# GpSimd instead of SP waits for the two result stores at the end of a decode kernel

## The chip, the core and the metric

The kernel runs on one core of one Trainium2 chip. A core has five engines with an instruction stream each: TensorE (PE; its weight loads are listed apart as PEld), VectorE (DVE), ScalarE (ACT), GpSimd (POOL) and SyncE (SP). They meet only at semaphores. Transfers are run by 16 DMA engines, and are issued here by SP and by ACT.

The metric is the device time of one execution, in microseconds (us). It covers a little more than the span of the profile, which goes from the first to the last instruction of the program: what the runtime does on every engine ahead of the program and behind it lies outside of the span.

## What is computed

One token goes through an attention block with a sliding window and, beside it, through a two-layer perceptron; both results and the input are added.

```python
xn = layernorm(x)                                   # x: 1 x 1024
q  = (xn @ wq) -> 32 heads x 128                    # wq: 1024 x 4096
k, v = last 4096 rows of the caches                 # 4 KV heads x 128, each shared by 8 heads
p  = softmax(q k^T / sqrt(128));  o = p v           # 32 heads
A  = o @ wo                                         # wo: 4096 x 1024
B  = gelu(layernorm(xn) @ w1 + b1) @ w2 + b2        # w1: 1024 x 3584, w2: 3584 x 1024
out = x + A + B                                     # 1 x 1024, bf16
```

## The kernel before

All weights and the part of the caches that is needed, 39.86 MB, are read once. SP issues these large loads; ACT issues the three small ones (b1, x and b2) at the start. Each load has a semaphore of its own, and each engine counts its results in a semaphore (the `Track` objects `PE`, `DVE`, `ACT`, `POOL`); a consumer waits for a count. There is no scheduler: the order of the work is the order in which the function writes it down, engine by engine.

In order of time: the small loads and the layer norms; the first perceptron layer as w1 lands; the gelu; the transposition of K on DVE; the queries as wq lands; scores, softmax and the second perceptron layer; the product with V; last, the output projection as wo lands. wo comes in four pieces of 20, 8, 3 and 1 of 32 columns of chunks (`WO_CHUNKS`), so that little is left to compute when the last piece has landed. All contributions to the result (x, b2, the perceptron, the attention) add up in one bank of PSUM as four quarter rows of 256.

GpSimd works at the start: constants, masks, a few products for the layer norms. Its last instruction (line 561) multiplies the sums of the softmax. From there to the end of the program its stream is empty.

The end (lines 621 to 631) works like this. The last matmul counts up the semaphore of PE (`C["fin"]`). PE ends with a branch at line 623 that is never taken. ACT waits for that count and copies the result out of PSUM to `ORow` as bf16 (line 627). Then ACT and SP each wait for ACT's count and each issue one store of 1 KB, half of the result; both stores add 16 to the semaphore `s_out` when they have landed (lines 628 to 630). SP then waits until `s_out` is 32 (line 631). This is the last instruction of the program on any engine.

Of the kernel before, what the change touches and what calls it, by code (L numbers as in the profile page):

```python
# [52 lines left out]
def bass_parallel_sum__sliding_block_cached__mixer_channel_mlp__decode_kernel(  # L53
# [18 lines left out]
    pe, dve, act, pool, sp = nc.tensor, nc.vector, nc.scalar, nc.gpsimd, nc.sync  # L72

    def sems(name, n):
        return [nc.alloc_semaphore(f"{name}{i}") for i in range(n)]

    s_xrow, s_b1, s_b2, s_w1, s_w2, s_out, s_go, s_row = (
        nc.alloc_semaphore(n) for n in ("s_xrow", "s_b1", "s_b2", "s_w1", "s_w2", "s_out", "s_go", "s_row"))
# [549 lines left out]
    for g, eng in enumerate((act, sp)):  # L628
        eng.wait_ge(ACT.sem, C["a_out"])
        eng.dma_start(out_rows[2 * g:2 * g + 2, :], ORow[31 + 64 * g:33 + 64 * g, :]).then_inc(s_out, 16)  # L630
    sp.wait_ge(s_out, 32)

    return nc

# [27 lines left out]
```

## Time and profile before

Three runs gave 99.16, 98.95 and 99.00 us, the median is 99.0 us. The profiled execution took 99.08 us.

| what | value |
|---|---|
| profiled execution, its own time | 99.08 us |
| its span, first to last instruction | 97.6 us (97.559) |
| outside of the span | 1.52 us |
| bytes read | 39.86 MB, 409 GB/s over the span |
| DMA's share of the chain that ended last | 88% |
| last matmuls on PE, start | 95.49 us |
| copy of the result on ACT, start and length | 95.81 us, 0.38 us |
| issue of the two stores, start and length | 96.22 us, 0.33 us on SP and 0.27 us on ACT |
| SP's wait for the stores | 1.0 us |
| last instruction on GpSimd, start and length | 72.24 us, 0.66 us |

The span ends with SP's wait. Semaphore instructions are not counted as busy, so the last microsecond looks empty in the table of busy time: only the list of SP's own waits shows it.

### The profile page before, as it was taken

The page shows a single profiled execution, that of the slowest core. Times are in us where ns is not written, and L with a number is a line of the kernel's source. Part 1 is how long each engine was busy: PE and PEld are TensorE (multiplying, and loading weights), DVE is VectorE, ACT ScalarE, POOL GpSimd, SP SyncE. Part 2 cuts the span into 40 slices and gives each one's busy share as a digit, 9 for nine tenths or more (in the row PEclk, how much of TensorE's full clock was granted, in tenths as well). Part 3 has the DMA queues.
Part 4 walks back from the last instruction along what each step waited for, and adds up shares of the span by engine and source line. Part 5 has one row for each costly group of instructions (what it writes and reads, how often), then busy time and mean ns, then how long its engine had stood idle before and what let it go on. Part 6 is the DMA issues. An engine that isn't in the chain of part 4 may idle for free.

```text
span 97.6 us, 1308 instructions
## 1 busy us (share of the span) xinstructions
PE 45.9 (47%) x527; PEld 19.8 (20%) x445; DVE 32.3 (33%) x43; ACT 12.3 (13%) x27; POOL 11.0 (11%) x31
## 2 busy tenths in 40 slices
PE   0000022649660000000069839993896499926962
PEld 0000022213120000000012122212544257603530
DVE  0000003270049999999900140416490000200000
ACT  0500000240320000000000130017680000100001
POOL 2000001499950000000000000000020000000000
PEclk9999999999998555555555799999579966997599
DMA  9798888999999999999898888999999699699980
GB/s 376 329 426 376 377 376 377 470 430 443 430 537 457 430 457 511 430 457 457 380 400 376 376 376 376 541 427 430 430 430 484 285 521 521 285 396 437 394 332 1
DMA packets 1340, 39.86 MB, mean 409 GB/s; under 512 B 182, under 2 KB 186, under 8 KB 444
## 3 DMA queue, kind: packets, MB, share of 16 engines
q1 hardware_dynamic: 1300, 39.85, 95.4%
q10 hardware_dynamic: 40, 0.01, 0.1%
HBM read 39.86 MB, written 0.00 MB: 409 GB/s over the span
## 4 chain that ended last, share of the span: by engine, by line
DMA 88%; PE 7%; SPq 2%; issue 1%; ACT 0%
DMA WW<-in_A_wq_dram 48%; DMA WW<-in_A_wo_dram 39%; PE PS L336 7%; SPq L199 1%; SPq L206 1%; SPq L214 0%; ACT ORow L627 0%; SPq L372 0%
## 5 line engine op out<-in xcount | busy, mean ns | idle before, releaser
L328 DVE STREAM_TRANSPOSE KV<-KV 128x2048 bf16<-128x2048 bf16 x8 | 18.5, 2312 | 0.3
L336 PE MATMUL PS<-WW,XNTb 128*32 x64 | 6.2, 574 | 20.3 <-SPq L372 20.3
L336 PE MATMUL PS<-WW,VEC 128*32 (+1 forms) x240 | 11.3, 337 | 4.6 <-SPq L610 3.1
L336 PEld LDWEIGHTS PS<-WW,VEC 128*32 (+1 forms) x236 | 6.0, 112 | 9.8 <-issue 8.8
L336 PE MATMUL PS<-KV,LB 128*128 128x512 bf16 x32 | 7.5, 386 | 0.7 <-DVE LB L452 0.7
L291 PE MATMUL PS<-oneb,XBR 1*128 1x1 bf16 x8 | 0.6, 194 | 13.8 <-DMA XBR<-in_A_x_dram 13.8
L336 PE MATMUL PS<-KV 128*64 x64 | 5.9, 345 | 2.1 <-DMA KV<-in_A_v_cache_dram 1.7
L336 PEld LDWEIGHTS PS<-WW,XNTb 128*32 x32 | 1.3, 126 | 25.5 <-issue 25.5
L336 PE MATMUL PS<-WW,YTb 128*32 x56 | 5.3, 507 | 1.6 <-DMA WW<-in_B_w_dram 1.6
L561 POOL TENSOR_TENSOR SUMX<-SAME,SUMP 128x128 f32<-128x128 f32 x1 | 0.7, 660 | 43.9 <-DVE SUMP L548 43.9
L294 DVE COPY XT<-PS 128x8 f32<-128x8 f32 x1 | 0.2, 168 | 14.4 <-PE PS L291 14.4
L336 PEld LDWEIGHTS PS<-KV 128*64 x64 | 3.9, 134 | 3.9 <-issue 3.3
L427 ACT ACTIVATE Hs<-PS 128x512 bf16<-128x512 f32 x1 | 0.6, 597 | 26.9 <-PE PS L336 26.9
L496 DVE TENSOR_REDUCE MXP<-PS 128x1 f32<-128x1024 f32 x2 | 2.4, 1224 | 4.5 <-PE PS L336 4.5
L592 DVE SCALAR_TENSOR_TENSOR OD<-PS,BLK,OD 128x128 f32<-128x128 f32 x1 | 0.3, 350 | 10.4 <-ACT OD L589 10.4
L291 PEld LDWEIGHTS PS<-oneb,XBR 1*128 1x128 bf16 x8 | 0.6, 160 | 13.8 <-issue 13.8
L429 DVE CAST Hs<-PS 128x512 bf16<-128x512 f32 x1 | 0.7, 691 | 7.2 <-PE PS L336 7.2
L545 DVE STREAM_TRANSPOSE KV<-KV 128x1024 bf16<-128x1024 bf16 x2 | 2.4, 1224 | 1.9 <-ACT KV L516 1.9
L516 ACT ACTIVATE KV<-PS,BIAS 128x512 bf16<-128x512 f32 x4 | 2.7, 682 | 0.1
L336 PEld LDWEIGHTS PS<-WW,YTb 128*32 x32 | 1.6, 111 | 5.6 <-issue 5.0
L336 PEld LDWEIGHTS PS<-KV,LB 128*128 128x128 bf16 x16 | 1.5, 96 | 5.6 <-issue 4.7
L221 POOL TENSOR_SCALAR_AFFINE_SELECT OUTM<-OUTM 2x512 bf16<-2x512 bf16 x1 | 2.3, 2303 | 0.1
(95 smaller groups left out, 42.3 us busy)
## 6 DMA issues: line engine op xcount, KB each, us to landing
WW<-in_B_w_dram SPq DMA_DIRECT2D x2, 7168.0 KB, 29.7
WW<-in_A_wo_dram SPq DMA_DIRECT2D x1, 5120.0 KB, 32.2
KV<-in_A_k_cache_dram SPq DMA_DIRECT2D x1, 4096.0 KB, 28.6
KV<-in_A_v_cache_dram SPq DMA_DIRECT2D x1, 4096.0 KB, 49.4
WW<-in_A_wo_dram SPq DMA_DIRECT2D x1, 2048.0 KB, 36.8
WW<-in_A_wo_dram SPq DMA_DIRECT2D x1, 768.0 KB, 38.2
WW<-in_A_wo_dram SPq DMA_DIRECT2D x1, 256.0 KB, 38.3
KV<-in_B_b_dram ACTq DMA_DIRECT2D x1, 7.0 KB, 8.8
```

The source lines that it names most:

```text
L199: sp.dma_start(dst[:, c0 * width:(c0 + n) * width].rearrange("p (c n) -> p c n", c=n), src[:, c0:c0 + n, :],).then_inc(semaphores[j], 16)
L206: sp.dma_start(dst[:, :], cache[0, :, SK - W:SK, :].rearrange("g (m b) d -> m g (b d)", m=MB),).then_inc(semaphore, 16)
L221: return POOL.mark(pool.affine_select(out=out, in_=out, pattern=pattern, compare_op=op, fill=value, base=base, channel_multiplier=step))
L291: last = pe.matmul(xt[:, r:r + 1], lhsT=XBR[0:1, r:D:KC], rhs=oneb[0:1, 0:1])
L328: C["kd"] = DVE.mark(dve.transpose(out=KD4[:, n], in_=KR[:, n * 2048:(n + 1) * 2048].rearrange("p (b e s) -> p b e s", b=16, e=4)))
L336: return pe.add_instruction(mybir.InstMatmult(name=nc.get_next_instruction_name(), engine=pe.engine, ins=[lowered(rhs, False), lowered(lhs ...
L427: C["a_qs"] = ACT.mark(act.activation(out=Qs[:, 0:512], in_=PS[:, 6 * 512:7 * 512], func=ACTF.Copy))
L429: C["d_qs"] = DVE.mark(dve.tensor_copy(Qs[:, 512:1024], PS[:, 7 * 512:8 * 512]))
L496: C["mx", i] = DVE.mark(dve.tensor_reduce(out=MXP[:, i:i + 1], in_=PS[:, i * 1024:(i + 1) * 1024], axis=AX.X, op=ALU.max))
L516: C["exp", n] = ACT.mark(act.activation(out=Pb[:, n * 512:(n + 1) * 512], in_=PS[:, n * 512:(n + 1) * 512], func=ACTF.Exp, bias=BIAS[:, i: ...
L545: C["tr", half] = DVE.mark(dve.transpose(out=PT[:, half * 1024:(half + 1) * 1024].rearrange("p (b m i g) -> p b m i g", b=HB, i=2, g=2), i ...
L561: C["sumx"] = POOL.mark(pool.tensor_tensor(out=SUMX[:, :].rearrange("p (g r) -> p g r", g=2), in0=SAME[:, :].unsqueeze(1).to_broadcast([12 ...
```

## The change

The instruction that waits until both stores have landed moves from SP's stream to GpSimd's. SP and ACT issue their stores as before. SP's stream now ends with the issue of its store (line 630), and GpSimd's, which ended with line 561, ends with the wait.

```diff
     for g, eng in enumerate((act, sp)):
         eng.wait_ge(ACT.sem, C["a_out"])
         eng.dma_start(out_rows[2 * g:2 * g + 2, :], ORow[31 + 64 * g:33 + 64 * g, :]).then_inc(s_out, 16)
-    sp.wait_ge(s_out, 32)
+    pool.wait_ge(s_out, 32)
 
     return nc
```

## The prediction

> **What bounds the kernel now.** I read the chain that ended last first. It says what the kernel is made of: 88% of it is the transfers of wq and wo, and at its end stand the last four matmuls and ACT's copy of the result.
>
> ```profile
> 57.13 38.31 DMA WW<-in_A_wo_dram
> 95.44 0.04 issue
> 95.49 0.30 PE PS L336 x4
> 95.78 0.02 issue
> 95.81 0.38 ACT ORow L627
> ```
>
> Nothing of this is touched. All that the change touches lies behind 96.2 us, so I read the order of events from 95 us on.
>
> ```profile
> 95.49 0.27 PE L336 MATMUL PS<-WW,VEC 128*32 128x256 bf16 x4
> 95.81 0.38 ACT L627 ACTIVATE ORow<-PS 128x256 bf16<-128x256 f32 x1 [12.35 <-PE PS L336]
> 96.22 0.33 SPq L630 DMA_DIRECT2D out_dram<-ORow  x1
> 96.22 0.27 ACTq L630 DMA_DIRECT2D out_dram<-ORow  x1
> ```
>
> The last row there starts at 96.22, the span ends at 97.56: the rest is a wait, which only SP's own list of waits shows, with its instruction under line 631.
>
> ```profile
> SPq L631 <- DMA out_dram<-ORow: 1.0, 1, 1.0
> ```
>
> ```profile
> L631 SPq EVENT_SEMAPHORE  x1: 17/17/17, 97.5 to 97.5; - x1
> ```
>
> So the span ends 17 ns after SP noticed that the stores had landed. GpSimd's list of waits shows it idle long before (its last instruction starts at 72.24 us):
>
> ```profile
> POOL SUMX L561 <- DVE SUMP L548: 43.9, 1, 43.9
> ```
>
> What follows the wait is outside of the span, but inside of the time: 99.08 - 97.56 = 1.52 us. No view prints it. The trace does keep the time of every write to a semaphore, and one semaphore that the program doesn't use (number 2) is counted up nine times in three rounds: just ahead of the first instruction, behind the last, and once more. These are rounds in which the engines meet. In us from the span's start:
>
> | step | ahead of the program | behind it | last round |
> |---|---|---|---|
> | 1 | -0.370 | 95.941 | 98.635 |
> | 2 | -0.336 | 96.849 | 98.669 |
> | 3 | -0.298 | 96.887 | 98.708 |
> | 4 | -0.254 | 96.931 | 98.752 |
> | 5 | -0.230 | 97.684 | 98.775 |
> | 6 | -0.119 | 97.727 | 98.873 |
> | 7 | -0.080 | 97.765 | 98.911 |
> | 8 | -0.046 | 97.799 | 98.945 |
> | 9 | 0.000 | 97.847 | 98.992 |
>
> The middle column tells who is who. Step 1 comes right after PE's last matmul has counted (95.78), step 2 after ACT's issue, steps 3 and 4 at once after it, by engines that had nothing left to do (POOL and DVE); then all stop until step 5, 0.125 us after SP's wait ended. Nine steps by five engines are a way up and a way down: PE, ACT, POOL, DVE, SP, DVE, POOL, ACT, PE. That POOL is third and DVE fourth I infer: semaphores are reset behind this round in five blocks, one per engine, and the blocks that start first after steps 6 and 7 are 156 to 206 and 105 to 155, ordered like the steps. From step 9 to the end of the last round is 1.145 us of resets and a second meeting. The last step, 98.99, lies 0.09 us short of the 99.08 us of this execution, so the time ends with this round, and whatever delays step 9 of the middle round delays the time.
>
> **The change part by part.**
>
> *Removed from SP.* SP's stream ends with the issue of its store (96.22 + 0.33 = 96.55). ACT, whose issue ends at 96.48, reaches its step at 96.85, 0.37 us later; SP likewise would be ready at about 96.92, 0.6 us ahead of the landing. SP comes off the path. Nothing is queued behind the wait on SP, and no DMA moves: both stores are issued as before, on the same two queues. Taken alone, this removes the SP tail: the wait's start is 17 ns after the last landing (97.525 to 97.542), step 5 comes 142 ns after that.
>
> *Added to POOL.* One semaphore instruction. Nothing of the program is queued behind it, and its place in the stream, behind line 561, is reached at 72.9 us: no engine waits for anything of POOL's after that. But its step 3 of the meeting is now late, and with it all behind it.
>
> *What is late next: the way through the meeting.* Before, the landing releases SP at the turning point; from step 5 to step 9 it takes 97.847 - 97.684 = 0.163 us. After, it releases POOL at step 3, and the count must go up to SP and down again. A round in which all are ready shows steps 3 to 9: 0.298 us ahead of the program (-0.298 to 0), 0.284 us in the last round (98.708 to 98.992). The difference is 0.121 to 0.135; I take the middle, 0.128 us. Most of it is the turn: step 5 to 6 takes 0.043 where DVE has been waiting (middle column), but 0.098 to 0.111 where the count comes straight up.
>
> The Trainium skill, page "Runtime: NRT & Kernel Launch", section "The launch sequence", gives this meeting as a serpentine over five engines with about 44 ns a hop. Released at step 3 in place of step 5, the count has two more hops to go: by that page an estimate of 0.088 us, and a sum smaller by 0.04 us. The trace's whole rounds of eight hops (0.370 and 0.357 us) agree with the page; its middle round, where a waiting DVE answers in 0.043 us, doesn't have the dear turn, and so I go by the trace.
>
> *What POOL itself needs.* Its tail, from the landing to its step, is not in this trace. Three parts by the nearest rows, in each case POOL against SP:
> - noticing: a POOL semaphore instruction in line 230 starts 32 ns after the DVE write it waits for (17.025 against 16.993), SP's 17 ns after the landing: +0.015.
> - going on to the next instruction: two such instructions of POOL in the preparation of the program follow each other by 79 ns; SP goes from its one there to its first DMA in 83 ns. No difference, or up to +0.03 if two instructions follow and SP's 142 ns hold two of 58: I take +0.015.
> - a drain, if each engine drains before it meets the others. SP's in the preparation takes 7 ns. POOL's takes 187 ns:
>
> ```profile
> L647 SPq DRAIN  x1: 7/7/7, 0.0 to 0.0; - x1
> L647 POOLq DRAIN  x1: 187/187/187, 0.4 to 0.4; - x1
> L647 POOL MEMSET const-uint8-127<- x1: 120/120/120, 0.4 to 0.4; 128x1 uint8 x1
> ```
>
> That drain waits for the memset, which starts at 0.39 and ends at 0.51; the drain ends at 0.56, some 0.05 behind it. With POOL long idle, the cost lies between SP's 0.007 and the whole 0.187; I take the 0.05 that it needs beyond the work it waits for, so +0.043 over SP.
>
> Could POOL be quicker than SP? Ahead of the program POOL starts its first instruction 0.215 us after its step 7, SP 0.230 after its step 5: -0.015 is the low end for the tail. The high end is 0.015 + 0.03 + 0.18 = +0.225.
>
> *Sum.* 0.128 (way) + 0.015 + 0.015 + 0.043 (tail) = +0.20 us; low end 0.121 - 0.015 = +0.11, high end 0.135 + 0.225 = +0.36. Against the profiled execution's own 99.08 that is 99.28; it lies 0.08 above the median of the runs, and the difference carried over to the median of 99.0 gives 99.20 us.
>
> **The rivals.** I count 0.2%, 0.2 us, as about what a measurement of this kernel can tell from no change; the three runs before lie 0.21 us apart.
>
> *1. POOL's tail is as short as SP's (not slower, by the bound).* Place: between the landing and step 3. If an idle POOL drains in 7 ns as SP does, the tail's surplus is -0.015 to +0.045, and only the way through the meeting is left: +0.11 to +0.18, so 99.15 us. For it speaks that four of five drains in the preparation take 7 to 10 ns; against it that the fifth is POOL's own. It decides from a drain under about 0.045 us on. If POOL stood at place 4 and DVE at 3, the way would be steps 4 to 9, 0.240 to 0.254, less 0.163: +0.08 to +0.09, which ends here too.
>
> *2. The store of SP lands sooner.* The two stores are issued together, but ACT's counts come at 97.328 and 97.341, SP's at 97.508 and 97.525. If SP's being busy with its wait on the same semaphore held up that landing by the 0.18 us, this is gained: 0.20 - 0.18 = +0.02, or 99.02 us; with the low end -0.07. Against it: SP's DMA engines finish their last packets 0.03 us behind ACT's, and an engine that only waits for a count has nothing to do with a write in flight. To end faster by over 0.2 us it would take more than this whole gap.
>
> *3. POOL's stream is slow to go on.* The whole 0.187 us for the drain gives +0.36, 99.36 us. Worse, POOL might have to fetch the runtime's instructions after a long wait; fetches ahead of the program last 0.34 to 0.56 us in the DMA's records: 99.6 to 99.8. But no such fetch is recorded after the other engines' last waits.
>
> *4. Nothing changes because the time ends elsewhere.* If the time were the span plus a constant, only the +0.015 of noticing would be seen: 99.02 us. Against it: the last step of the meeting meets the measured time to 0.09 us.
>
> **How the numbers follow.** The forecast 0.43 and rival 3 0.11; rival 1: 0.28; rival 4: 0.05; rival 2: 0.05; 0.08 are left for a gain that no row explains. Slower by over 0.2%: the forecast lies on the bound itself; I count it as slower, since all that isn't in the rows of POOL (a drain, a fetch) can only add, and rival 3 with it: 0.54. Same: 0.28 + 0.05 + 0.05 = 0.38. Faster: 0.08. The likeliest gives 99.20 us, by itself from 99.11 to 99.36. The range takes in rivals 1 and 2 and the drain's high end, with 0.08 us for the scatter of runs (the profiled execution's distance from the median): from 99.02 - 0.08 = 98.94 to 99.36 + 0.08 = 99.44.
>
> **What the profile afterwards would show.** The wait appears under line 631 on POOL, not on SP, with 17 ns, some 1.0 us after the stores are issued; the span stays at 97.6 us within 0.1. SP's last instruction is the store at 96.2. In the record of semaphore 2, steps 1 and 2 stay where they are, step 3 follows the wait's end by 0.125 us or more (POOL's tail), steps 3 to 9 take 0.28 to 0.30 us in place of the 0.163 of steps 5 to 9, and the time outside of the span grows from 1.52 to 1.7 us. A step 3 that comes 0.12 us after the wait speaks for rival 1, one later than 0.25 for rival 3, an SP store landing with ACT's for rival 2. I am wrong if steps 3 and 4 come ahead of the wait's end, for then POOL isn't where I put it.

## The result and the profile after

With GpSimd waiting, the median is 99.43 us (99.36 to 99.84, 7 runs), against 99.0 us before (98.91 to 99.19, 7 runs): a ratio of 1.0051, 95% interval 1.0036 to 1.0066, or +0.50 us (+0.36 to +0.65). The kernel became slower, as forecast, and 99.43 lies just inside of the range, whose upper end is 99.44; but the change is two and a half times the +0.20 us of the forecast.

The span didn't grow: it is 97.58 us in the profiled execution after, 97.56 before. The end of the program looks as it did, in the timeline of the changed kernel (start, length, engine, line, operation):

```profile
95.50 0.27 PE L336 MATMUL PS<-WW,VEC 128*32 128x256 bf16 x4
95.82 0.38 ACT L627 ACTIVATE ORow<-PS 128x256 bf16<-128x256 f32 x1 [12.37 <-PE PS L336]
96.23 0.33 SPq L630 DMA_DIRECT2D out_dram<-ORow  x1
96.23 0.27 ACTq L630 DMA_DIRECT2D out_dram<-ORow  x1
```

At this end of the program the wait has moved, and nothing else. Line 631 of the changed kernel, with the duration in ns three times and the start in us:

```profile
L631 POOLq EVENT_SEMAPHORE  x1: 17/17/17, 97.6 to 97.6; - x1
```

SP's list of waits has lost the 1.0 us for the stores, and its wait for ACT's copy is its last one in the program (the last row is the preparation ahead of it):

```profile
SPq L630 <- ACT ORow L627: 3.2, 1, 3.2
SPq L647 <- PEq L647: 0.7, 1, 0.7
```

No row of the page shows where half a microsecond went, for it went behind the span. The time that runs of before spend outside of their span is 1.38 us in the mean (32 runs that were timed beside the first experiments, 1.20 to 1.54); with the change it is 1.86 us (7 runs, 1.76 to 2.04). What is in it, the trace tells by its times of writes to semaphore 2, as in the prediction. In us from each span's start, for the middle round of the meeting:

| | before | after |
|---|---|---|
| last of the stores' counts | 97.525 | 97.540 |
| the wait's row, start to end | 97.542 to 97.559 (SP) | 97.564 to 97.581 (POOL) |
| step 1, PE | 95.941 | 95.953 |
| step 2, ACT | 96.849 | 96.860 |
| step 3, POOL | 96.887 | 98.119 |
| step 4, DVE | 96.931 | 98.162 |
| step 5, SP | 97.684 | 98.185 |
| step 6, DVE | 97.727 | 98.283 |
| step 7, POOL | 97.765 | 98.321 |
| step 8, ACT | 97.799 | 98.355 |
| step 9, PE | 97.847 | 98.402 |

The reader is to see two gaps. Before, the round stands still between steps 4 and 5, until SP has noticed the stores; after, between steps 2 and 3, until POOL has. And from the end of the wait's row to that engine's step it is 0.125 us on SP, but 0.538 us on POOL. From the last count to step 9 it takes 0.322 us before and 0.862 after: +0.540 us, inside of the measured interval.

### The profile page after: what moved, and what is told of

Its sections match the earlier page's. It is cut to its first block, busy times and chain, and to the rows that moved or that the text cites. A ratio compares the mean times of both kernels' runs of the same rounds, so it can differ in the third digit from the quotient of the medians.

```text
span 97.6 us, 1308 instructions
## 1 busy us (share of the span) xinstructions
PE 45.6 (47%) x527; PEld 20.0 (21%) x445; DVE 32.2 (33%) x43; ACT 12.3 (13%) x27; POOL 11.0 (11%) x31
## 4 chain that ended last, share of the span: by engine, by line
DMA 89%; PE 6%; SPq 2%; issue 1%; ACT 0%
DMA WW<-in_A_wq_dram 49%; DMA WW<-in_A_wo_dram 40%; PE PS L336 6%; SPq L199 1%; SPq L206 1%; SPq L214 0%; ACT ORow L627 0%; SPq L372 0%
## 5 line engine op out<-in xcount | busy, mean ns | idle before, releaser
L336 PE MATMUL PS<-WW,XNTb 128*32 x64 | 5.2, 496 | 19.7 <-SPq L372 19.7
L336 PE MATMUL PS<-WW,YTb 128*32 x56 | 5.9, 554 | 1.5 <-DMA WW<-in_B_w_dram 1.5
```

What stands on the lines that cost most here:

```text
L336: return pe.add_instruction(mybir.InstMatmult(name=nc.get_next_instruction_name(), engine=pe.engine, ins=[lowered(rhs, False), lowered(lhs ...
```

## The experiments

**Who waits.** Theory A, formed from these two columns: the loss is POOL's own way from its wait to its step (call it the tail), plus the longer way through the meeting. Its first rival B says that SP alone is quick and any other engine pays the same; rival C, that the loss comes from taking SP's wait away, not from giving one to POOL. Each of the first three kernels is the one line with another engine, for instance

```diff
-    sp.wait_ge(s_out, 32)
+    dve.wait_ge(s_out, 32)
```

> DVE waits for the two stores, nobody else. Theory A (the additional time with GpSimd is its own long way from the wait to its step in the meeting, 0.54 us against SP's 0.125, plus the longer way through the meeting): DVE's tail is like SP's, it is released at step 4, steps 4 to 9 take 0.24 to 0.25 us in place of 0.163, so +0.08 to +0.09 us against before, about 99.1 us, no difference that a measurement tells. Theory B (SP alone is quick; any engine that waits at the end pays some 0.54 us for its tail): +0.50 us, 99.5 us.

> ACT waits for the two stores, nobody else. Theory A: released at step 2, steps 2 to 9 take 0.32 to 0.34 us in place of 0.163, ACT's tail is like SP's: +0.17 us, 99.17 us. Theory B: +0.17 + 0.41 = +0.58 us, 99.6 us.

> PE waits for the two stores, nobody else. Theory A: released at step 1, the whole round of 0.36 to 0.37 us in place of 0.163, tail like SP's: +0.20 us, 99.2 us. Theory B: +0.20 + 0.41 = +0.61 us, 99.6 us.

The fourth keeps SP's wait and adds POOL's:

```diff
     sp.wait_ge(s_out, 32)
+    pool.wait_ge(s_out, 32)
```

> SP keeps its wait and GpSimd has the same wait as well: the added part of the change alone. Theory A: GpSimd's tail is the longer one and hides SP's; step 3 comes 0.54 us behind the wait as with the change, +0.5 us, 99.45 us. Rival C (the time is lost because SP no longer waits, for instance by what its stream does behind its store): near before, within 0.1 us of 99.0 us.

Measured, each against before on the same chip (median 99.01 us, 32 runs; the last row is the result above, against 99.0 us), beside what the semaphore times of the profiled execution say. "Last count" is the last of the stores' counts on `s_out`:

| who waits | median us | ratio, 95% interval | last count to that engine's step | that step to step 9 | last count to step 9, against before |
|---|---|---|---|---|---|
| DVE | 99.16 | 1.0009 (0.9996 to 1.0022) | 0.189 (step 4) | 0.240 | +0.107 |
| ACT | 99.22 | 1.0020 (1.0005 to 1.0035) | 0.152 (step 2) | 0.322 | +0.152 |
| PE | 99.21 | 1.0022 (1.0011 to 1.0032) | 0.267 (step 1) | 0.355 | +0.300 |
| SP and POOL | 99.40 | 1.0043 (1.0028 to 1.0058) | 0.578 (step 3) | 0.285 | +0.541 |
| SP (before) | | 1 | 0.159 (step 5) | 0.163 | 0 |
| POOL (after) | 99.43 | 1.0051 (1.0036 to 1.0066) | 0.579 (step 3) | 0.283 | +0.540 |

B falls: ACT and DVE have SP's tail within 0.03 us, PE is 0.11 us slower, POOL 0.42. C falls: with SP's wait still in place, the whole loss is there. Theory A's times for DVE, ACT and PE came out; PE's with some luck, since its way to its step is 0.11 us longer than A took it, and the measured interval (+0.11 to +0.32 us) holds both the +0.20 expected and the +0.300 of the trace. The two waits of the kernel that has both, from its profile:

```profile
L631 SPq EVENT_SEMAPHORE  x1: 17/17/17, 97.5 to 97.5; - x1
```

```profile
L632 POOLq EVENT_SEMAPHORE  x1: 17/17/17, 97.6 to 97.6; - x1
```

Both engines notice the stores at the same moment (17 and 24 ns after the last count, by the trace's times); SP is ready when its turn comes (step 5 follows step 4 by 24 ns), and the round waits for POOL. The three kernels also settle who stands where: the step that comes late is the fourth with DVE, the second with ACT, the first with PE, and the third with POOL, as the prediction had inferred.

The Trainium skill, page "Runtime: NRT & Kernel Launch", section "The launch sequence", gives about 0.355 us for a whole round, the one ahead of a program. With PE waiting, steps 1 to 9 take 0.355 us here, so trace and page agree.

**What POOL's tail is.** Three explanations can be tried: a drain that is long on POOL (D, against E: the tail belongs to the end of POOL's stream), a POOL that is slow because it stood still for 24 us (F), and a fetch of instructions (G). In all three kernels POOL alone waits. These kernels, and the one with two semaphores that follows them, were measured against before on another chip (median 98.93 us, 12 runs). For D:

```diff
-    sp.wait_ge(s_out, 32)
+    pool.wait_ge(ACT.sem, C["a_out"])
+    pool.drain()
+    pool.drain()
+    pool.wait_ge(s_out, 32)
+    pool.drain()
+    pool.drain()
```

> GpSimd alone waits for the stores; two drains are put into its stream ahead of that wait (at 96.2 us, hidden) and two behind it (on the path). Theory D (the 0.54 us from GpSimd's wait to its step are a drain that takes some 0.4 us on an idle GpSimd): each drain row lasts about 0.4 us, and the two behind the wait bring the time to 99.45 + 0.8 = 100.2 us. Theory E (a drain of an idle GpSimd is as short as on the others, the 0.54 us are something that only the end of its stream has): drain rows of 0.01 to 0.05 us, the two add 0.1 to 0.2 us, 99.6 us.

Measured: 99.72 us, ratio 1.0067 (1.0044 to 1.0091). The drains' own lines; the first and the third hold the waits:

```profile
L632 POOLq DRAIN  x1: 41/41/41, 96.4 to 96.4; - x1
...
L633 POOLq DRAIN  x1: 34/34/34, 96.5 to 96.5; - x1
...
L635 POOLq DRAIN  x1: 34/34/34, 97.8 to 97.8; - x1
...
L636 POOLq DRAIN  x1: 34/34/34, 97.8 to 97.8; - x1
```

An idle POOL drains in 34 ns: not the 0.4 us of D, and a little under the 0.05 us of the prediction. From the last count to step 3 it is 0.648 us, 0.07 more than with the change, about what the two drains add: POOL's last row ends 0.119 us behind the last count here, 0.041 with the change. From the end of the last drain to step 3 there are still 0.529 us. D falls, as far as a drain that the program writes tells of one behind it.

For F, POOL gets a short fill just ahead of the wait:

```diff
-    sp.wait_ge(s_out, 32)
+    pool.wait_ge(ACT.sem, C["a_out"])
+    pool.memset(SUMX[:, 0:1], 0.0)
+    pool.wait_ge(s_out, 32)
```

> GpSimd alone waits for the stores, but is given a short fill of one column at 96.2 us, just ahead of the wait, so that it isn't idle for 24 us before. Theory F (GpSimd is slow to go on because it stood still for so long): its step 3 comes 0.15 to 0.25 us behind the wait, time near 99.15 us. Theory A with a fixed tail: step 3 comes 0.54 us behind the wait as with the change, 99.45 us.

Its profile shows POOL at work 1.3 us before the wait ends:

```profile
96.39 0.10 POOL L632 MEMSET SUMX<- 128x1 f32 x1 [21.69 <-ACT ORow L627]
```

Step 3 comes 0.578 us after the last count, 0.537 after the wait's end: F falls for the long standstill; POOL is still idle for 1.2 us between the fill and the end of the wait. The median is 99.69 us, ratio 1.0071 (1.0049 to 1.0094, 4 runs). That is above the forecast, though +0.54 us lies inside of the interval; the trace shows nothing longer than with the change.

For G, 100 empty instructions stand ahead of the wait:

```diff
-    sp.wait_ge(s_out, 32)
+    for _ in range(100):
+        pool.nop(nofuse=True)
+    pool.wait_ge(s_out, 32)
```

> GpSimd alone waits for the stores; 100 empty instructions stand ahead of the wait, done long before, so that the end of its stream lies elsewhere in the instruction memory. Theory G (the 0.54 us are a fetch of the instructions behind the wait): the tail changes by 0.3 us or more one way or the other, 99.1 or 99.8 us. Fixed tail: 0.54 us behind the wait, 99.45 us.

99.52 us, ratio 1.0052 (1.0032 to 1.0071); step 3 is 0.578 us behind the last count. Neither with the change nor here does the trace have a fetch at the end of the span. But this test is weaker than the others. The trace has no row for the empty instructions (it has one for each of SP's three), so that they moved the end is known from the source alone; and the last fetch of 8 KB in any trace here starts 7.7 us ahead of the span, so that none at its end says little. What speaks against G most is that POOL's tail is 0.537 or 0.538 us in every kernel that ends POOL's stream with a wait, while the recorded fetches of 8 KB last from 0.31 to 0.63 us. G is unlikely, not excluded.

The last question is whether POOL's tail begins with its wait, or waits for something else that ends at about the same time. Here each store has its own semaphore, and POOL waits for ACT's store alone (the line that allocates `s_out2` is not shown):

```diff
-        eng.dma_start(out_rows[2 * g:2 * g + 2, :], ORow[31 + 64 * g:33 + 64 * g, :]).then_inc(s_out, 16)
-    sp.wait_ge(s_out, 32)
+        eng.dma_start(out_rows[2 * g:2 * g + 2, :], ORow[31 + 64 * g:33 + 64 * g, :]).then_inc((s_out, s_out2)[g], 16)
+    sp.wait_ge(s_out2, 16)
+    pool.wait_ge(s_out, 16)
```

> Each store has a semaphore of its own: GpSimd waits for ACT's store alone (it lands 0.18 us earlier), SP for its own. Theory A with a fixed tail: step 3 comes at the landing of ACT's store, 97.34, plus 0.54 us, that is 0.18 us earlier than with the change, and SP's wait is hidden behind it: +0.32 us against before, 99.32 us. Rival H (GpSimd's step waits for something else that ends at about 98.1 us in all kernels): as with the change, 99.45 us.

The two waits, SP's at line 632 and POOL's at 633:

```profile
L632 SPq EVENT_SEMAPHORE  x1: 17/17/17, 97.7 to 97.7; - x1
...
L633 POOLq EVENT_SEMAPHORE  x1: 17/17/17, 97.5 to 97.5; - x1
```

POOL's wait ends at 97.523, its step 3 comes at 98.060: again 0.537 us, though it was released 0.18 us ahead of SP. H falls. The time is 99.39 us, ratio 1.0049 (1.0029 to 1.0068); that interval holds both the +0.32 us expected and the +0.50 of the change, so it is the trace that decides here, not the time.

**A shorter end?** In all these kernels ACT's store counts 0.18 us ahead of SP's. If the second store is what is late, a single one would end sooner. Its four rows are 32 partitions apart, where the same quarter rows lie:

```diff
-    for g, eng in enumerate((act, sp)):
-        eng.wait_ge(ACT.sem, C["a_out"])
-        eng.dma_start(out_rows[2 * g:2 * g + 2, :], ORow[31 + 64 * g:33 + 64 * g, :]).then_inc(s_out, 16)
-    sp.wait_ge(s_out, 32)
+    act.wait_ge(ACT.sem, C["a_out"])
+    act.dma_start(out_rows, ORow[0:128:32, :]).then_inc(s_out, 16)
+    sp.wait_ge(s_out, 16)
```

> One store of all four quarter rows (from four rows of the result tile that are 32 partitions apart), issued by ACT; SP waits for it alone. In all kernels so far ACT's store landed 0.18 us ahead of SP's. Theory I (SP's store is late because it is SP's, or because it is the second on its way): the one store lands 1.12 us after the start of its issue as ACT's does, the wait and the whole end come 0.18 us sooner, 98.83 us. Rival J (it is late because four rows have to land, whoever sends them): no change against before, 99.0 us.

> The same one store issued by SP, which also waits for it. If SP's queue is the slow one: as before, 99.0 us. If only the second store is late: 0.18 us sooner, 98.83 us.

Both expectations missed: 99.30 us twice against 99.08 us of before on the same chip, ratios 1.0027 (1.0015 to 1.0040) with ACT and 1.0025 (1.0011 to 1.0040) with SP. Most of it is the issue, in the timeline of the one and of the other:

```profile
96.33 0.60 ACTq L629 DMA_DIRECT2D out_dram<-ORow  x1
```

```profile
96.42 0.65 SPq L629 DMA_DIRECT2D out_dram<-ORow  x1
```

Four rows 32 partitions apart take 0.60 and 0.65 us to issue, where the two stores of two neighbouring rows took 0.27 and 0.33 side by side. From the start of the issue to the last count it is 1.65 and 1.67 us, in place of 1.31 before; from its end to the last count it is 1.05 and 1.02, in place of 0.98 for SP's store before. Whether the number of the rows or the distance between them is to blame was not taken apart, and why SP's store counts 0.18 us behind ACT's these two kernels cannot tell. No kernel here beats the one before.

## Why the prediction was right or wrong

- *What bounds the kernel, and where the time goes:* right. The span is the same within 0.02 us; all of the loss lies behind the span, between the wait and the end of the engines' meeting.
- *Removed from SP:* right. Nothing was queued behind the wait, no transfer moved, and both stores count at the same distance from their issue as before. What SP gives up is covered by POOL's longer tail, as the kernel with both waits shows.
- *The way through the meeting, +0.128 us:* right. 0.283 us from step 3 to step 9 against 0.163 from step 5, so +0.120; with ACT, DVE and PE the same table gave the right lengths too. That POOL stands third and DVE fourth came true as well, but not for the reason given: the blocks of resets don't begin in the order of the steps. Behind step 7 (97.765) 207 to 255 begins first (97.804), then 156 to 206 (97.871), 54 to 104 (97.904) and only then 105 to 155 (97.917). The experiments show the places.
- *Noticing, +0.015:* 24 ns against 17 after the last count, so +0.007.
- *POOL's tail behind the wait, +0.015 and +0.043, high end +0.21:* this is the term that failed. It measured 0.538 against SP's 0.125, so +0.413, about twice the high end. The high end was taken from POOL's longest drain, and the drain is not the cost: idle, it takes 34 ns. The prediction took it for granted that the tail is made of a few instructions such as the preparation shows, and priced it by their rows; in fact 0.53 us lie between the last instruction of POOL that the trace shows and its step, whatever that last instruction is (semaphore instruction or drain), and on ACT and DVE some 0.11 and 0.14. What fills them isn't recorded. A drain that the program writes, the long idleness and another event were tried and excluded, a fetch made unlikely. Nor is POOL slow in all it does behind the program: if each of the five blocks of resets is one engine's, POOL's own, whichever it is, begins within 0.30 us of its step 7 (98.321 in the trace after; the last block begins at 98.618). What remains is that the 0.53 us come with the end of POOL's stream, which is only argued, and their cause stays open.
- *Sum:* 0.120 + 0.007 + 0.413 = +0.540 by the trace, +0.50 (0.36 to 0.65) by the times, where +0.20 stood. That 99.43 still lies inside of the range is luck: its upper end was made of POOL's longest drain, which is not what POOL spends the time on, and of 0.08 us for scatter.
- *The time ends with the last step of the last round:* wrong. After, that step comes at 99.55 us, 0.18 us behind the profiled execution's own 99.37. The 0.09 us that spoke for it before were an accident of one execution: in the twelve profiled executions here the last step lies from 0.09 us ahead of the execution's own time to 0.18 behind it, in eight of them 0.18 behind, and outside of the span runs of before scatter by 0.34 us. Shifts of step 9 do follow the measured differences in all kernels above, within their intervals.
- *The rivals:* rival 1 (a short tail) and rival 4 (nothing outside of the span counts) fell by the table; rival 2 fell, since ACT's counts come at 97.356 and SP's at 97.540, 0.18 us apart as before. Rival 3 (POOL's stream is slow to go on) is what came, by the sign named for it, a step 3 later than 0.25 us after the wait; it had 0.11 of the chance. Neither of its two reasons was borne out: the drain's +0.36 us was too little and the drain is short, and of the fetch, at 99.6 to 99.8 us, nothing is recorded.

## What to carry to other kernels

In this kernel the last wait decided on which engine the end begins, and the end had a price of its own that no row of the profile's page shows: compare the time with the span, and look at who is released last. Here SP was the cheapest engine to wait on, DVE couldn't be told from it, ACT and PE cost 0.2% more, and GpSimd 0.5%; an engine that has been idle for long, and so looks free, isn't for that reason the cheap one. For an operation whose cost is nowhere in the trace, a high end from the nearest row is no bound when the row is of another operation.

## What was not expected of the hardware

- GpSimd took 0.537 to 0.538 us from the end of its last wait to its step in the engines' meeting in all five kernels in which its stream ended with a wait; SP took 0.125, ACT 0.113, DVE 0.140 and PE 0.187. What fills the difference is not recorded.
- An idle GpSimd drains in 34 ns; most of the 187 ns of its drain ahead of the program (0.37 to 0.56 us) lie beside a fill that ends at 0.51.
- A store of four rows 32 partitions apart took 0.60 to 0.65 us to issue, about twice that of two neighbouring rows (0.27 to 0.33 us), and its count came 0.34 us later.
